# Attention probabilities of the later half blocks: 32x32 block turns on VectorE and a way through DRAM in place of TensorE transposes

## The chip, the cores and the metric

The kernel runs on one core of a Trainium2 chip. The metric is the device time of one execution in microseconds (us); the kernel before takes 675.06 us, the median of three runs (675.04 to 675.08).

## The reference

Four batches of 8 heads, 768 positions and 64 dimensions go through an attention with a window of 16 on either side and 24 block summaries. The result, 3072 tokens of 512, goes through a two-layer network of 512 to 2048 to 512 with a rational function between the layers.

```python
k_sum = k.reshape(B, H, nb, block, D).max(axis=3)          # block = 32, nb = 24
v_sum = v.reshape(B, H, nb, block, D).mean(axis=3)
scores_l = where(|i - j| < 16, scale * q @ k.T, -1e9)
scores_s = scale * einsum('bhsd,bhnd->bhsn', q, k_sum) + log(block)
a = softmax(concatenate([scores_l, scores_s], axis=-1))    # +1e-9 below
x = (a @ concatenate([v, v_sum], axis=2)), heads side by side: [3072, 512]
h = x @ w_in
P = a[0] + a[1]*h + a[2]*h**2 + a[3]*h**3
Q = 1 + |b[0]|*|h| + |b[1]|*h**2
out = (P / (Q + 1e-6)) @ w_out
```

## The kernel before

**Attention.** The 3072 queries are cut into 48 half blocks of 64 (`HQ`). A half block sees `NK` = 120 keys: 96 of its window and 24 summaries. Its scores for all 8 heads stand in one PSUM tile `sc` of 128 rows (2 heads x 64 queries) and 4 x 120 columns (4 head pairs). `scores` (line 195) is a generator in five pieces: TensorE (PE) computes `sc`; VectorE (DVE) adds the mask, scales and takes the smallest value, into `ss` in SBUF; ScalarE (ACT) takes the exponential and the sum `sm`; DVE inverts `sm`; GpSimd (POOL) multiplies `ss` by it. For the product with the values the probabilities must stand with the keys on the partitions: `turned` (line 241) does this with four PE transposes into the PSUM tile `pt`, one per head pair, and `copied` (line 279) has ACT copy `pt` into `pts`. `both_values` (line 284) then multiplies two half blocks by their values `vw` into one tile `av` of PSUM and copies that into the tokens `x`.

**Network.** The tokens go in 6 groups of 512 and each group through 16 steps of 128 hidden columns, 96 steps in all. A step is 12 matmuls for the first layer (`moe1`, tile `h`) and 12 for the second (`moe2`, four tiles `po`), which runs three steps behind (`LAG`). Each layer is three products of parts in high and low precision. Between them `gelu` evaluates the rational function: ACT squares and scales, DVE runs six operations of 128x512 on `tq`, `tu` and `gh`, ACT runs a logarithm and an exponential, and POOL makes `gl`. The PSUM banks of `h` are two, and `av` takes its turn among them; `sc` and `pt` have two of their own, `po` has four.

**Where the two meet.** Half blocks 0 to 15 are done early. The 32 later ones are taken in pairs: the two of a pair are scored at step 14 + 4k (k from 0 to 15) and multiplied by their values four steps later, so one pair falls to every four steps. From step 14 on (`NSTRICT`) a scheduler orders each engine's instructions at build time, with a raised priority for scores, loads and values. The transposes of a pair are put between the second layer's matmuls of the two steps after next: `turned_copied` (line 472) is handed to `moe2` (line 403), which puts one transpose ahead of every three matmuls, the first half block's in step 14 + 4k + 2, the second's one step on. `Kept` (line 75) passes every operation on, so all of them carry its line, 85, and are told apart by their tiles. All loads and stores of this phase are issued by SyncE (SP) in one queue: the next pair's `qw` and `kw` (`att_load`, line 185), its `vw` (`load_v`, line 230), summaries, and the output.

Of the kernel before, what the change touches and what calls it, by code (L numbers as in the profile page):

```python
# [22 lines left out]
P = 128  # L23
# [7 lines left out]
NK = NKW + NB  # L31
NKC = NK // NB
GT = 512
NG = NT // GT
# [16 lines left out]
EARLY_HALF = (0, 1, 3, 4, 6, 7, 9, 10)  # L51
NSTRICT = NFC - 2
STEP = "h3 k0 h0 l0 a0 g1 h1 w2 h1 g1 h3 h0 g0 q0 w2 u g0 q0 w3 g1 h0 w2 w3 P2 v h2"
NHALF = NT // HQ
# [3 lines left out]
def tile_kernel(ctx, tc, qw_in, kraw, kwin, vpad, vred, wio, a, b, cmask, cident, cavg, out):  # L58
# [136 lines left out]
    def scores(jj, early=False):  # L195
# [15 lines left out]
        pool, tag = (gp, "gl") if early and jj % 2 else (pp, "p")  # L211
        ss = pool.tile([P, NPAIR, NK], F32, tag=tag, name=f"ss{jj}")
        sm = sp.tile([P, 2, NPAIR], F32, tag="sm", name=f"sm{jj}")
        for pr in range(NPAIR):
            dve.tensor_tensor_reduce(
                out=ss[:, pr, :], in0=sc[:, pr * NK:(pr + 1) * NK], in1=mt, op0=ALU.add, op1=ALU.min,
                scale=-SCALE, scalar=3.0e38, accum_out=sm[:, 0, pr:pr + 1])
        yield
        for pr in range(NPAIR):
            act.activation(ss[:, pr, :], ss[:, pr, :], AF.Exp, scale=-1.0,  # L220
                           bias=sm[:, 0, pr:pr + 1], accum_out=sm[:, 1, pr:pr + 1])
        act.activation(sm[:, 1, :], sm[:, 1, :], AF.Copy, bias=1e-9)
        yield
        dve.reciprocal(sm[:, 1, :], sm[:, 1, :])
        yield
        for pr in range(NPAIR):
            gps.tensor_scalar(ss[:, pr, :], ss[:, pr, :], sm[:, 1, pr:pr + 1], 1.0, op0=ALU.mult, op1=ALU.mult)
        att[jj] = ss
# [49 lines left out]

    def copied(jj):
        pt = att[jj]  # L280
        att[jj] = pp.tile([NK, NPAIR, P], F32, tag="p", name=f"pts{jj}")
        act.copy(att[jj], pt[:NK, :].rearrange("k (r q) -> k r q", r=NPAIR))

    def both_values(j0):
# [5 lines left out]
        for k in range(2):  # L290
            pts = att.pop(j0 + k)
            for pr in range(NPAIR):
                for e in range(2):
                    pe.matmul(
                        av[e * D:(e + 1) * D, pr, k, :],
                        vw[k][:, (2 * pr + e) * D:(2 * pr + e + 1) * D],
                        pts[:, pr, e * HQ:(e + 1) * HQ], start=True, stop=True)
        act.copy(x32[g][:, :, hh * HQ:(hh + 2) * HQ], av.rearrange("p r k q -> p r (k q)"))
# [104 lines left out]
    def moe2(fc, po, gh, gl, between):  # L403
        wt = weights(fc)
        for t in range(TPG):
            with tc.high_priority(offset=40):
                next(between, None)
            ts_ = slice(t * P, (t + 1) * P)
# [13 lines left out]
    def second_layer(step, queue, po, pt):  # L422
# [7 lines left out]
        return po  # L430

    vnext = tc.dram_tile([NB, DM], F32, name="vnext")
    vres = vw + [mp.tile([NK, DM], F32, tag=t, name=f"vr{i}") for i, t in enumerate(("ta", "tq", "ta", "tq"))]
# [29 lines left out]
    def lead(chain, all_of=False):  # L463
        for _ in chain or ():
            if not all_of:
                return

    def finish_half(jj, early, copy=None):
        lead(turned(jj, early), True)
        return values(jj, early, copy)  # L470

    def turned_copied(jj):
        yield from turned(jj)
        copied(jj)

# [47 lines left out]
    for step in range(NG * NFC + LAG):  # L523
# [54 lines left out]
        with tc.high_priority(offset=40):  # L578
            if step - 4 >= NFC - 2 and halves.get(step - 4):
                both_values(halves[step - 4][0])  # L580
            for jj in halves.get(step, ()):
                key_blocks(jj)
                lead(scores(jj), True)
            for jj in halves.get(step, ()):
                load_v(jj)
                if jj + 2 < NHALF:
                    att_load(jj + 2)
        pt = (z for k in range(2) for jj in halves.get(step - 2 - k, ())[k:k + 1] if jj >= 2 * HPG for z in turned_copied(jj))
        po = second_layer(step, queue, po, pt)
        with tc.high_priority(offset=40):  # L590
            lead(pt, True)
        for f, *args in reduces.get(step, []) + loads.get(step, []):
# [57 lines left out]
```

## Time and profile before

| | before |
|---|---|
| median of 3 runs | 675.06 us |
| the profiled execution's own time | 674.83 us |
| its span, first to last instruction | 673.0 us |
| TensorE clock granted, mean | 0.986 |
| TensorE (PE) busy | 655.2 us, 97% |
| VectorE (DVE) busy | 574.9 us, 85% |
| ScalarE (ACT) busy | 473.7 us, 70% |
| GpSimd (POOL) busy | 263.6 us, 39% |
| DMA | 60.75 MB, mean 90 GB/s |

Busy time is the time in which an engine had an instruction in work. The profiled execution is one run; what lies between its span and its time, 1.8 us, is outside the first and the last instruction.

### The profile page before, as it was taken

How to read it: one execution, taken by the hardware profiler on the slowest of the kernel's cores; microseconds unless marked ns; L12 is line 12 of the kernel's file. 1: busy time of each engine (PE TensorE's matmuls, PEld its weight loads, DVE VectorE, ACT ScalarE, POOL GpSimd, SP SyncE). 2: the span in 40 equal slices, each digit the busy share in tenths (PEclk: the TensorE clock that was granted, in tenths of full speed). 3: DMA queues.
4: the chain of work that ended last, by engine and by line, in shares of the span. 5: the costliest groups of instructions: out<-in, count | busy, mean ns of one | idle time of the engine just before them, and what ended most of it. 6: DMA issues, size and time to landing. Idle time of an engine off the chain costs nothing.

```text
span 673.0 us, 11873 instructions
## 1 busy us (share of the span) xinstructions
PE 655.2 (97%) x4196; PEld 522.7 (78%) x4196; DVE 574.9 (85%) x1116; ACT 473.7 (70%) x1068; POOL 263.6 (39%) x318
## 2 busy tenths in 40 slices
PE   8897989998999999999999999999999999999997
PEld 5675767776878888888888888888788788888886
DVE  4579999998899989977889988878987778988885
ACT  3869879877867668766667677567686576675563
POOL 1736566835334145244244234333442342222221
PEclk9988989999999999999999999999999999999999
DMA  9997644311224302212114222012031000010001
GB/s 322 331 299 243 221 157 146 140 49 62 94 79 118 127 23 70 67 60 64 56 33 132 87 87 69 21 44 63 0 127 64 0 25 1 1 63 1 0 1 63
DMA packets 29671, 60.75 MB, mean 90 GB/s; under 512 B 3636, under 2 KB 15284, under 8 KB 27692
## 3 DMA queue, kind: packets, MB, share of 16 engines
q1 hardware_dynamic: 28908, 59.54, 27.1%
q8 instruction: 33, 0.54, 0.3%
q10 hardware_dynamic: 576, 0.25, 0.2%
q14 instruction: 26, 0.21, 0.1%
q0 software_dynamic: 128, 0.20, 0.1%
HBM read 53.44 MB, written 6.34 MB: 89 GB/s over the span
## 4 chain that ended last, share of the span: by engine, by line
PE 82%; DVE 8%; DMA 3%; ACT 3%; issue 2%; POOL 1%; SPq 0%; DVEq 0%; ACTq 0%
PE po L85 36%; PE h L85 34%; PE sc L85 6%; PE av L85 3%; PE pt L85 3%; DVE tu L85 2%; DMA wr<-in_wio_dram 2%; DVE tq L85 2%; DMA kres<-in_kraw_dram 1%; DVE wr L85 1%; DVE gh L85 1%; PE vf L85 1%; ACT ta L85 1%; ACT ss L85 1%; DVE w L85 1%
## 5 line engine op out<-in xcount | busy, mean ns | idle before, releaser
L85 POOL TENSOR_TENSOR gl<-tu,ta 128x512 fp32r<-128x512 f32 x96 | 128.3, 1337 | 289.9 <-DVE tu L85 159.9
L85 POOL TENSOR_SCALAR ss<-ss,sm 128x120 f32<-128x120 f32 x192 | 107.1, 579 | 101.5 <-DVE sm L85 101.3
L85 DVE SCALAR_TENSOR_TENSOR tq<-tq,cs,ta 128x512 f32<-128x512 f32 x96 | 106.3, 1107 | 38.9 <-ACT ta L85 38.3
L85 ACT ACTIVATE tq<-h 128x512 f32<-128x512 f32 x96 | 57.2, 596 | 107.1 <-PE h L85 104.3
L85 PE MATMUL po<-wearly,gh 128*128 128x512 f32 x384 | 130.2, 421 | 0.0
L85 PE MATMUL po<-w,gh 128*128 128x512 f32 x384 | 126.7, 411 | 0.0
L85 ACT ACTIVATE ta<-tq,cs 128x512 f32<-128x512 f32 x96 | 69.7, 726 | 50.0 <-DVE tq L85 49.5
L85 PE MATMUL h<-xh,wearly 128*128 128x512 f32 x384 | 96.8, 393 | 1.7 <-DVE tu L85 1.1
L85 PE MATMUL h<-xh,w 128*128 128x512 f32 x384 | 95.1, 390 | 0.0
L85 DVE SCALAR_TENSOR_TENSOR gh<-tu,cs,ta 128x512 fp32r<-128x512 f32 x96 | 77.5, 807 | 18.5 <-ACT ta L85 9.9
L85 PEld LDWEIGHTS h<-xh,wearly 128*128 128x128 f32 x384 | 71.7, 188 | 19.9 <-DVE tu L85 1.6
L85 PEld LDWEIGHTS h<-xh,w 128*128 128x128 f32 x384 | 72.1, 188 | 15.5
L85 ACT ACTIVATE ss<-ss,sm 128x120 f32<-128x120 f32 x192 | 73.3, 386 | 10.8 <-DVE sm L85 10.0
L85 PEld LDWEIGHTS po<-wearly,gh 128*128 128x128 f32 x384 | 66.4, 193 | 17.7 <-issue 2.6
L85 PEld LDWEIGHTS po<-w,gh 128*128 128x128 f32 x384 | 65.9, 189 | 16.9 <-issue 1.3
L85 PE MATMUL po<-w,gl 128*128 128x512 f32 x192 | 75.4, 392 | 1.0 <-POOL gl L85 1.0
L85 PE MATMUL po<-wearly,gl 128*128 128x512 f32 x192 | 76.2, 397 | 0.0
L85 ACT ACTIVATE tu<-h,cs 128x512 f32<-128x512 f32 x96 | 74.9, 781 | 0.0
L85 DVE SCALAR_TENSOR_TENSOR tu<-tu,cs,tq 128x512 f32<-128x512 f32 x96 | 72.0, 750 | 2.7
L85 DVE SCALAR_TENSOR_TENSOR tu<-tu,cs,h 128x512 f32<-128x512 f32 x96 | 71.4, 744 | 2.2
L85 DVE SCALAR_TENSOR_TENSOR tq<-tq,gh 128x512 f32<-128x512 f32 x96 | 66.6, 694 | 3.2
L85 ACT ACTIVATE ta<-h,cs 128x512 f32<-128x512 f32 x96 | 65.5, 682 | 4.2 <-POOL gl L85 4.2
(68 smaller groups left out, 972.1 us busy)
## 6 DMA issues: line engine op xcount, KB each, us to landing
wr<-in_wio_dram SPq DMA_DIRECT2D x15, 1024.0 KB, 6.9
vw<-in_vpad_dram SPq DMA_DIRECT2D x42, 192.0 KB, 2.8
kw<-in_kwin_dram SPq DMA_DIRECT2D x40, 192.0 KB, 3.3
out_dram<-o SPq DMA_DIRECT2D x24, 256.0 KB, 2.1
qw<-in_qw_dram SPq DMA_DIRECT2D x40, 128.0 KB, 3.2
kr<-in_kraw_dram SPq DMA_DIRECT2D x12, 384.0 KB, 3.0
vr<-in_vred_dram SPq DMA_DIRECT2D x8, 384.0 KB, 3.4
vf<-in_vpad_dram SPq DMA_DIRECT2D x2, 1024.0 KB, 12.2
```

The lines of the kernel that those rows point to most:

```text
L85: out = getattr(self.engine, name)(*args, **kw)
```

## The change

For the 32 later half blocks `ss` is widened to 128 columns, of which POOL clears the last eight. The two score chains of a pair run piece by piece side by side, where before one followed the other. One step after the scores (`CROSS`) `crossed` has DVE turn `ss` in blocks of 32x32 into `tb`: within each block queries and keys change places, and the blocks stay where they are. To bring the blocks to their rows, `tb` is written to DRAM (`cross`, 256 KB, one of four places in turn) and read back in four pieces, one for each 32 keys (the last 24), each with 64 KB or less in runs of 512 B, into `pts`, which has two buffers of its own. Writes and reads are issued by SP. The matmuls of `both_values` read `pts` as two runs of 32 columns. The PE transposes and ACT copies of these half blocks are gone; the early half blocks keep theirs.

```diff
--- before.py
+++ after.py
@@ -30,6 +30,8 @@
 NKW = HQ + 2 * WIN
 NK = NKW + NB
 NKC = NK // NB
+SQ = 32
+NKB = -(-NK // SQ)
 GT = 512
 NG = NT // GT
 HPG = GT // HQ
@@ -50,6 +52,7 @@
 NSTG = 8
 EARLY_HALF = (0, 1, 3, 4, 6, 7, 9, 10)
 NSTRICT = NFC - 2
+CROSS = 1
 STEP = "h3 k0 h0 l0 a0 g1 h1 w2 h1 g1 h3 h0 g0 q0 w2 u g0 q0 w3 g1 h0 w2 w3 P2 v h2"
 NHALF = NT // HQ
 
@@ -209,22 +212,24 @@
                     pe.matmul(sc[rows, pr * NK + lo:pr * NK + hi], qt[rows, pr, :], k[rows], start=True, stop=True)
         yield
         pool, tag = (gp, "gl") if early and jj % 2 else (pp, "p")
-        ss = pool.tile([P, NPAIR, NK], F32, tag=tag, name=f"ss{jj}")
+        ss = pool.tile([P, NPAIR, P], F32, tag=tag, name=f"ss{jj}")[:, :, 0:NK if jj < 2 * HPG else P]
         sm = sp.tile([P, 2, NPAIR], F32, tag="sm", name=f"sm{jj}")
         for pr in range(NPAIR):
             dve.tensor_tensor_reduce(
-                out=ss[:, pr, :], in0=sc[:, pr * NK:(pr + 1) * NK], in1=mt, op0=ALU.add, op1=ALU.min,
+                out=ss[:, pr, 0:NK], in0=sc[:, pr * NK:(pr + 1) * NK], in1=mt, op0=ALU.add, op1=ALU.min,
                 scale=-SCALE, scalar=3.0e38, accum_out=sm[:, 0, pr:pr + 1])
         yield
         for pr in range(NPAIR):
-            act.activation(ss[:, pr, :], ss[:, pr, :], AF.Exp, scale=-1.0,
+            act.activation(ss[:, pr, 0:NK], ss[:, pr, 0:NK], AF.Exp, scale=-1.0,
                            bias=sm[:, 0, pr:pr + 1], accum_out=sm[:, 1, pr:pr + 1])
         act.activation(sm[:, 1, :], sm[:, 1, :], AF.Copy, bias=1e-9)
         yield
         dve.reciprocal(sm[:, 1, :], sm[:, 1, :])
         yield
+        if jj >= 2 * HPG:
+            gps.memset(ss[:, :, NK:], 0.0)
         for pr in range(NPAIR):
-            gps.tensor_scalar(ss[:, pr, :], ss[:, pr, :], sm[:, 1, pr:pr + 1], 1.0, op0=ALU.mult, op1=ALU.mult)
+            gps.tensor_scalar(ss[:, pr, 0:NK], ss[:, pr, 0:NK], sm[:, 1, pr:pr + 1], 1.0, op0=ALU.mult, op1=ALU.mult)
         att[jj] = ss
 
     def load_v(jj):
@@ -276,10 +281,18 @@
             yield
             dve.tensor_tensor(xl[:, :, cols], av, xh[:, :, cols], op=ALU.subtract)
 
-    def copied(jj):
-        pt = att[jj]
-        att[jj] = pp.tile([NK, NPAIR, P], F32, tag="p", name=f"pts{jj}")
-        act.copy(att[jj], pt[:NK, :].rearrange("k (r q) -> k r q", r=NPAIR))
+    def crossed(jj):
+
+        ss = att[jj]
+        tu = pp.tile([P, NKB, NPAIR, SQ], F32, tag="p", name=f"tb{jj}")
+        dve.transpose(out=tu.rearrange("p n r q -> p r n q"), in_=ss.rearrange("p r (n q) -> p r n q", q=SQ))
+        nc.sync.dma_start(out=cross[jj % 4], in_=tu)
+        att[jj] = pp.tile([NK, P // SQ, NPAIR, SQ], F32, tag="pts", name=f"pts{jj}", bufs=2)
+        for n in range(NKB):
+            k = min(SQ, NK - n * SQ)
+            nc.sync.dma_start(
+                out=att[jj][n * SQ:n * SQ + k],
+                in_=cross[jj % 4][:, n].rearrange("(b a) r q -> a b r q", a=SQ)[0:k])
 
     def both_values(j0):
 
@@ -292,9 +305,9 @@
             for pr in range(NPAIR):
                 for e in range(2):
                     pe.matmul(
-                        av[e * D:(e + 1) * D, pr, k, :],
+                        av[e * D:(e + 1) * D, pr, k, :].rearrange("d (b q) -> d b q", q=SQ),
                         vw[k][:, (2 * pr + e) * D:(2 * pr + e + 1) * D],
-                        pts[:, pr, e * HQ:(e + 1) * HQ], start=True, stop=True)
+                        pts[:, 2 * e:2 * e + 2, pr, :], start=True, stop=True)
         act.copy(x32[g][:, :, hh * HQ:(hh + 2) * HQ], av.rearrange("p r k q -> p r (k q)"))
 
     def split(g):
@@ -404,7 +417,7 @@
         wt = weights(fc)
         for t in range(TPG):
             with tc.high_priority(offset=40):
-                next(between, None)
+                lead(between)
             ts_ = slice(t * P, (t + 1) * P)
             for i, (l, r) in enumerate(((gh, 0), (gh, 1), (gl, 0))):
                 pe.matmul(po[t], l[:, ts_], wt[:, r, 1, :], start=(fc == 0 and i == 0),
@@ -429,6 +442,7 @@
                 finish(g, po)
         return po
 
+    cross = [tc.dram_tile([P, NKB, NPAIR, SQ], F32, name=f"cross{i}") for i in range(4)]
     vnext = tc.dram_tile([NB, DM], F32, name="vnext")
     vres = vw + [mp.tile([NK, DM], F32, tag=t, name=f"vr{i}") for i, t in enumerate(("ta", "tq", "ta", "tq"))]
     vlast = stage.tile([NK, 2, DM], F32, tag="st", name="vlast")
@@ -468,10 +482,6 @@
     def finish_half(jj, early, copy=None):
         lead(turned(jj, early), True)
         return values(jj, early, copy)
-
-    def turned_copied(jj):
-        yield from turned(jj)
-        copied(jj)
 
     def whole(jj):
         yield from scores(jj)
@@ -580,15 +590,18 @@
                 both_values(halves[step - 4][0])
             for jj in halves.get(step, ()):
                 key_blocks(jj)
-                lead(scores(jj), True)
+            chain = [scores(jj) for jj in halves.get(step, ())]
+            for _ in range(5):
+                for c in chain:
+                    lead(c)
+            for jj in halves.get(step - CROSS, ()):
+                if jj >= 2 * HPG:
+                    crossed(jj)
             for jj in halves.get(step, ()):
                 load_v(jj)
                 if jj + 2 < NHALF:
                     att_load(jj + 2)
-        pt = (z for k in range(2) for jj in halves.get(step - 2 - k, ())[k:k + 1] if jj >= 2 * HPG for z in turned_copied(jj))
-        po = second_layer(step, queue, po, pt)
-        with tc.high_priority(offset=40):
-            lead(pt, True)
+        po = second_layer(step, queue, po, None)
         for f, *args in reduces.get(step, []) + loads.get(step, []):
             f(*args)
```

In the following pieces a name ends in a running number; `ss_3320` and `ss_3345` before are `ss_3357` and `ss_3363` in the changed kernel.

On PE, in step 8 of the third group, which is two steps after a pair's scores, this stands before:

```order
L85 MATMUL h_8_3421<-xh_2882,w_1106 128x512 x8
L85 MATMUL h_8_3421<-xl_2883,w_1106 128x512 x4
L85 MATMUL pt_3451<-ident,ss_3320 120x128
L85 MATMUL po_0_3149<-wearly,gh_5_3227 128x512 x2
L85 MATMUL po_0_3149<-wearly,gl_5_3228 128x512
L85 MATMUL pt_3451<-ident,ss_3320 120x128
L85 MATMUL po_1_3150<-wearly,gh_5_3227 128x512 x2
L85 MATMUL po_1_3150<-wearly,gl_5_3228 128x512
```

and this in the changed kernel:

```order
L88 MATMUL h_8_3467<-xh_2920,w_1110 128x512 x8
L88 MATMUL h_8_3467<-xl_2921,w_1110 128x512 x4
L88 MATMUL po_0_3191<-wearly,gh_5_3262 128x512 x2
L88 MATMUL po_0_3191<-wearly,gl_5_3263 128x512
L88 MATMUL po_1_3192<-wearly,gh_5_3262 128x512 x2
L88 MATMUL po_1_3192<-wearly,gl_5_3263 128x512
```

Four such transposes to a half block are gone, 128 in all; nothing else on PE has moved.

On DVE, from the end of step 6 of the same group (`sm` is the two halves' sum, `gh`, `tq` and `tu` with their step's number are the rational function), before:

```order
L85 SCALAR_TENSOR_TENSOR gh_6_3276<-tu_6_3280,cs,ta_6_3278 128x512
L85 SCALAR_TENSOR_TENSOR tq_6_3279<-tq_6_3279,gh_6_3276 128x512
L85 RECIPROCAL sm_3321<-sm_3321 128x4
L85 RECIPROCAL sm_3346<-sm_3346 128x4
L85 SCALAR_TENSOR_TENSOR tu_6_3280<-tu_6_3280,cs,tq_6_3279 128x512
L85 SCALAR_TENSOR_TENSOR tq_7_3395<-tq_7_3395,cs,ta_7_3394 128x512
L85 TENSOR_TENSOR tu_7_3396<-tu_7_3396,h_7_3379 128x512
L85 SCALAR_TENSOR_TENSOR tu_7_3396<-tu_7_3396,cs,h_7_3379 128x512
L85 SCALAR_TENSOR_TENSOR gh_7_3392<-tu_7_3396,cs,ta_7_3394 128x512
```

and now:

```order
L88 SCALAR_TENSOR_TENSOR gh_6_3304<-tu_6_3308,cs,ta_6_3306 128x512
L88 SCALAR_TENSOR_TENSOR tq_6_3307<-tq_6_3307,gh_6_3304 128x512
L88 RECIPROCAL sm_3358<-sm_3358 128x4
L88 RECIPROCAL sm_3364<-sm_3364 128x4
L88 SCALAR_TENSOR_TENSOR tu_6_3308<-tu_6_3308,cs,tq_6_3307 128x512
L88 STREAM_TRANSPOSE tb_3439<-ss_3357 128x4x4x32
L88 SCALAR_TENSOR_TENSOR tq_7_3425<-tq_7_3425,cs,ta_7_3424 128x512
L88 STREAM_TRANSPOSE tb_3447<-ss_3363 128x4x4x32
L88 TENSOR_TENSOR tu_7_3426<-tu_7_3426,h_7_3409 128x512
L88 SCALAR_TENSOR_TENSOR tu_7_3426<-tu_7_3426,cs,h_7_3409 128x512
L88 SCALAR_TENSOR_TENSOR gh_7_3422<-tu_7_3426,cs,ta_7_3424 128x512
```

Two transposes have come in, one on either side of the first operation of step 7, and ahead of the two products `tu` with `h`; the multiplication of `ss` by POOL comes before each.

On SP, from the loads of the next pair's queries and keys, before:

```order
L187 DMA qw_98<-in_qw_dram 128x256
L188 DMA kw_96<-in_kwin_dram 128x384
L187 DMA qw_99<-in_qw_dram 128x256
L188 DMA kw_97<-in_kwin_dram 128x384
L233 DMA vw_100<-in_vpad_dram 96x512
L233 DMA vw_101<-in_vpad_dram 96x512
```

and now:

```order
L190 DMA qw_98<-in_qw_dram 128x256
L191 DMA kw_96<-in_kwin_dram 128x384
L190 DMA qw_99<-in_qw_dram 128x256
L191 DMA kw_97<-in_kwin_dram 128x384
L289 DMA cross_109<-tb_3439 128x512
L289 DMA cross_110<-tb_3447 128x512
L293 DMA pts_3442<-cross_109 32x4x128 x3
L293 DMA pts_3442<-cross_109 24x4x128
L293 DMA pts_3450<-cross_110 32x4x128 x3
L293 DMA pts_3450<-cross_110 24x4x128
L238 DMA vw_100<-in_vpad_dram 96x512
L238 DMA vw_101<-in_vpad_dram 96x512
```

Two writes and eight reads stand between those loads and the loads of the values; the writes wait for DVE, and the first read of each tile for its write's landing.

## Rows read from the trace of the kernel before

**Rows 1.** Part 1 of the page: busy us (share of the span) xinstructions of each engine

```profile
PE 655.2 (97%) x4196; PEld 522.7 (78%) x4196; DVE 574.9 (85%) x1116; ACT 473.7 (70%) x1068; POOL 263.6 (39%) x318
```

**Rows 2.** Chain that ended last, one period: start us, us, what

```profile
201.00 1.08 PE av L85 x32
202.09 1.79 PE sc L85 x32
203.87 2.95 PE po L85 x12
206.82 2.72 PE h L85 x12
209.54 2.72 PE po L85 x12
...
214.99 0.11 PE pt L85
215.10 0.70 PE po L85 x3
```

**Rows 3.** Busy time by stretch of one period: each engine's us, then clock and DMA

```profile
149.08:175.04 25.96, 23.84 (x106) 18.06 (x106) 23.27 (x51) 19.49 (x45) 10.96 (x13) 1.00 0.18 56
...
201.00:226.96 25.96, 25.96 (x171) 21.07 (x172) 24.78 (x47) 17.62 (x41) 8.73 (x12) 1.00 0.34 103
226.96:252.92 25.96, 25.96 (x171) 21.08 (x172) 23.21 (x49) 17.29 (x41) 8.74 (x12) 1.00 0.23 71
252.92:278.88 25.96, 25.96 (x171) 21.07 (x172) 24.07 (x47) 19.49 (x45) 12.72 (x14) 1.00 0.15 46
...
356.76:382.72 25.96, 25.96 (x171) 21.08 (x172) 24.94 (x49) 19.37 (x45) 10.63 (x12) 1.00 0.35 100
...
460.60:486.56 25.96, 25.96 (x171) 21.08 (x172) 23.28 (x46) 19.59 (x45) 11.14 (x12) 1.00 0.14 41
...
sum 389.40, PE 389.40 PEld 316.18 DVE 332.73 ACT 273.56 POOL 141.87; mean PE 25.96 PEld 21.08 DVE 22.18 ACT 18.24 POOL 9.46
```

**Rows 4.** All instructions of tile pt: ns min/median/max, first and last start us

```profile
L85 PE MATMUL pt<-ident,ss x192: 270/271/469, 17.9 to 560.8; 128*120 128x128 f32 x192
```

**Rows 5.** DVE groups by form, 201 to 564 us: busy, mean ns | idle before

```profile
L85 DVE SCALAR_TENSOR_TENSOR tq<-tq,cs,ta 128x512 f32<-128x512 f32 x56 | 61.1, 1091 | 29.9 <-ACT ta L85 29.7
...
L85 DVE TENSOR_TENSOR tu<-tu,h 128x512 f32<-128x512 f32 x56 | 37.9, 677 | 0.0
```

**Rows 6.** The same view over the whole run

```profile
L85 DVE MEMSET zero<- 128x512 f32 x1 | 0.5, 485 | 0.9 <-PEq L639 0.9
```

**Rows 7.** DVE in order of time: start us, us, instruction [idle before <-releaser]

```profile
280.13 1.39 DVE L85 SCALAR_TENSOR_TENSOR tq<-tq,cs,ta 128x512 f32<-128x512 f32 x1 [0.60 <-ACT ta L85]
...
289.22 0.75 DVE L85 SCALAR_TENSOR_TENSOR tq<-tq,cs,ta 128x512 f32<-128x512 f32 x1 [0.88 <-ACT ta L85]
289.95 0.69 DVE L85 TENSOR_TENSOR tu<-tu,h 128x512 f32<-128x512 f32 x1
```

**Rows 8.** POOL in order of time, the same stretch

```profile
279.70 1.27 POOL L85 TENSOR_TENSOR gl<-tu,ta 128x512 fp32r<-128x512 f32 x1 [3.07 <-DVE tu L85]
...
288.27 3.30 POOL L85 TENSOR_SCALAR ss<-ss,sm 128x120 f32<-128x120 f32 x8
```

**Rows 9.** DVE in order of time, a period with a value reduction

```profile
224.54 0.75 DVE L85 SCALAR_TENSOR_TENSOR tu<-tu,cs,h 128x512 f32<-128x512 f32 x1
```

**Rows 10.** DMA issues: x issues, KB each, median us from issue to landing

```profile
out_dram<-o SPq DMA_DIRECT2D x24, 256.0 KB, 2.1
qw<-in_qw_dram SPq DMA_DIRECT2D x40, 128.0 KB, 3.2
...
vr<-in_vpad_dram SPq DMA_DIRECT2D x4, 192.0 KB, 12.5
```

**Rows 11.** SP in order of time: start us, us, issue

```profile
279.54 0.80 SPq L233 DMA_DIRECT2D vw<-in_vpad_dram  x2
...
281.37 0.42 SPq L188 DMA_DIRECT2D kw<-in_kwin_dram  x1
```

## The prediction

> **What bounds the kernel now.** I read the shares of the engines first, then the chain of waits over one period, then the busy time period by period, and last the order in time around the places that change. TensorE is busy for 97% of the span and VectorE for 85% [rows 1], so a saving on the one is a load on the other, and where each stands matters. From the second pair of half blocks on the work repeats every four steps, in 25.96 us. The chain of such a period is all PE: the values of one pair, 1.08 us; the scores of another, 1.79; a second layer of 2.95; first and second layers of 2.72 each; and, in two of the second layers, four transposes that hold the chain for 0.11 us each and stretch the three matmuls behind them to 0.70 [rows 2], where three matmuls of an undisturbed layer take 2.72 / 4 = 0.68. The stretches say the same: in each of the 15 periods from 175.04 to 564.44 us PE is busy for all of 25.96 us, 389.40 in sum, at the full granted clock, and VectorE for 22.18 in the mean [rows 3]. So in these 389 us nothing but PE counts, and VectorE has 3.8 us to spare per period in the mean, but far less in some: 24.78, 23.21 and 24.07 in three that follow one another, 24.94 and 23.28 in two more [rows 3]. These hold reductions of keys and values and the splits of a new group. The period before, in which the first pair's transposes stand, has PE busy for 23.84 of 25.96 us [rows 3]: there others are waited for.
>
> **What PE gains.** A transpose takes some 271 ns by itself [rows 4], but most of that lies beside other matmuls; what counts is the chain. Without transposes a period is 1.08 + 1.79 + 2.95 + 7 x 2.72 = 24.86 us, which is 1.10 less than 25.96. For 15 pairs that is 16.5 us. The first pair's gain lies between nothing (PE waits there anyway) and 1.1; I take half, 0.5. Together 17.0, and 674.83 - 17.0 = 657.8 us for the profiled execution, whose time stands 0.23 below the median of the runs; I forecast against it and leave that difference to the range.
>
> **What VectorE pays.** Each half block brings one turn of 128x512. The trace has no such instruction. Nearest is an operation of one output of that size, `tu` times `h`, at 677 ns; a clearing of the same size, which reads nothing, took 485 ns, the lower end [rows 5, 6]. I know nothing that makes a turn dearer than twice a product, 1.35 us, and take that as the upper end, the product as the value: in, out and elements are as many. To the work comes a wait. Replay the period from 278.88: POOL begins the eight multiplications at 288.27 and ends them at 291.57, 0.41 each, so the first half block's four end at 289.92 [rows 8]. The first turn stands ahead of step 7's `tq`, which began at 289.22, and the second behind it, ahead of `tu` times `h` at 289.95 [rows 7]. Now: first turn 289.92 to 290.59, `tq` to 291.34, second turn from 291.57, when POOL is done, to 292.24, and only then `tu` times `h`. That is 2.3 us later: 1.34 of work and 1.0 of waiting for POOL. Behind it stand the rest of that step's function and the next one's.
>
> Whether PE feels it: it needs the two products with `h` to free a bank of `h`, and `gh` and `gl` three steps later. The three steps cover several microseconds; the bank covers less. In the period to 226.96 the last product ended at 225.29, 1.67 ahead of the values that take its bank [rows 9]; with the 0.54 us that four transposes less bring PE forward, 1.1 is left. Charge every period 2.3: the mean becomes 24.5 of 24.86, which fits, so in a light period the delay is made up before the next pair. The heavy ones exceed 24.86 by 2.22, 0.65 and 1.51 (in a row), 2.38, and 0.72. Take from each run of heavy periods the 1.1 that the bank covers: 3.3 + 1.3 + 0 = 4.6 us lost, if nothing is given back. Something will be: `tq` takes 1.39 us where it runs beside POOL's `gl` and 0.75 where it does not [rows 7, 8], 1.09 in the mean [rows 5]; four of them in a period hold 1.4 us that a later, back-to-back VectorE need not lose, enough for all of the excess. I take the middle, 2.5 us lost, with 0 and 4.6 as ends at this price of a turn.
>
> The Trainium skill speaks against this change: "VectorE: DVE Perf Modes", section "The three transpose paths", gives TensorE 390 ns for 128x128 in bf16 and VectorE 311, the latter in separate blocks of 32x32 only, and its "Rules for kernel authors" leave 128x128 turns to TensorE where PSUM will do as the target. Four such squares would be 1.24 us a half block by that figure (an estimate; the data here are fp32), and the sum some 665 us. In the trace here a transpose on TensorE costs its chain 0.14 us, 1.10 / 8, less than half of the page's figure.
>
> **The transfers.** They lie beside everything, if they land in time. For the same period: second turn done at 292.24, its write issued in some 0.4 us [rows 11] and landed 2.1 later, as the output's stores of the same 256 KB do [rows 10], at 294.7; the first tile's write and reads are through by then or queued ahead on SP; the second tile's four reads are issued one after another at 0.42 us, to 296.5, and land 3.3 us later, a little over the 3.2 of `qw` [rows 10]: 299.8. The values of this pair start on PE at 278.88 + 24.86 = 303.74. That leaves 3.9 us. What is queued on SP behind the writes and reads is the loads of `vw`, which cannot start before the preceding values anyway, next `qw` and `kw`, and stores of the output, whose buffers are needed 16 steps later: no cost. The upper end for a landing is the slowest small load of the trace, 12.5 us [rows 10], at the busy start.
>
> **What I cost at nothing.** ACT loses 32 copies and is busy 18.24 of 25.96 us [rows 3]: off the path on either side of the change. POOL gains 32 clearings of 128x4x8, at 9.46 of 25.96 us busy [rows 3]; they wait only for a buffer and lie in POOL's idle time; if they did not, each would push the turns by less than a multiplication's 0.41. The interleaved score chains bring the first half block's probabilities no later than POOL's order above has them. The values' matmuls read two runs of 32 columns instead of one of 64; the scores already read keys in runs of 24 and run 32 matmuls in 1.79 us [rows 2], so I give it nothing.
>
> Sum: 674.83 - 17.0 + 2.5 = **660.3 us**.
>
> **The rivals.**
> *VectorE becomes the bound.* If a turn costs 1.35 us, a period's charge is 2.3 + 2 x 0.67 = 3.65, the mean 25.8 against 24.86. VectorE then sets the pace in all but the lightest periods. Over the 15 stretches the excess comes to about 16 us after the banks' 1.1 per run of periods; with nothing given back that is 657.8 + 16 = 674, with 1.4 per heavy period given back 661 to 662; I take 668. For it: VectorE's 85%, its FIFO order, and that the turn writes in an order of its own, 32 by 32. Against: rows of 0.68 to 0.75 for every plain operation of that size.
> *Transfers land late, and the kernel gets slower.* The reads come in pieces of 512 B. If they land not 3.3 but over 8.3 us after issue, the 3.9 us of slack and the 1.1 of gain are gone, and each period is longer than before. PE would wait at `av`, and as the next pair's scores stand behind `av`, the delay would come back in each period. At 12.5 us, `av` starts 5.3 late: 15 x 5.3 = 80, and 657.8 + 80 = 738 us. For it: the one row at 12.5. Against: 2.1 to 3.2 us for loads and stores of this phase [rows 10], and DMA engines busy for 0.14 to 0.35 of the stretches shown [rows 3].
> *No effect.* The saved time reappears as waiting of PE on `gl` or `h`, whatever the turn's price, since VectorE's chain after the scores is longer by 2.3 us in every period and no light one makes it up: about 675. Against: PE waits for nothing in 389 us, so VectorE keeps a reserve throughout.
>
> **How the numbers follow.** Forecast 0.60; VectorE as the bound 0.27; late transfers 0.08; no effect 0.05. A measurement of this kernel can tell a change of 0.2%, 1.35 us, so faster means under 673.7 and slower over 676.4. The forecast and nearly all of the second rival are faster: 0.86. Same takes most of no effect and a little of the second: 0.05; slower the rest: 0.09. The range goes from 656.0 (a turn at 485 ns, nothing lost, the first pair's whole 1.1 gained, and the period before it a little shorter) to 671.0, which takes in the middle and the upper part of the second rival and leaves out late transfers, no effect and the tail of VectorE, some 0.17.
>
> **What would show it.** Right: no `pt` after the first sixteen half blocks; a period of 24.9 us in the light stretches, with PE busy throughout; a turn's row near 0.68 us; idle time of VectorE of about 1 us per period ended by POOL's `ss`; waits of PE for VectorE's `tu` or POOL's `gl` of some 2.5 us in sum, near the stretches that are now at 201 to 279 and 357 to 383 us; reads landed 3 us or more ahead of `av`. Wrong: a turn of over 1 us and VectorE busy for over 97% of each period; waits of PE at `av` that a transfer of `pts` ends; or waits for `h` in the light periods too.

## The result and the profile after

The changed kernel takes 665.8 us (median of 4 runs, 665.17 to 666.42), beside 675.05 for the kernel before in the same series (674.99 to 675.08): a ratio of 0.9863, 95% interval 0.9846 to 0.988. That is 9.3 us faster where 14.5 were forecast. The profiled execution took 665.17 us with a span of 663.4.

What follows speaks of periods: the time from the first values matmul of one pair of later half blocks to that of the next. Period 1 begins with the values of the first such pair, at 174.25 us in the changed kernel, and holds the scores and the turns of the second; period 15 ends with the values of the sixteenth, at 554.78. The splits of a new group (`xh` and `xl`) stand in periods 4, 8 and 12. The busy time of each engine by period, for the kernel after (columns as in [rows 3]):

```profile
174.25:200.00 25.75, 25.36 (x161) 20.43 (x161) 21.90 (x46) 18.30 (x43) 9.96 (x14) 1.00 0.42 137
200.00:226.39 26.39, 24.94 (x161) 20.59 (x161) 26.00 (x51) 17.62 (x41) 10.30 (x16) 1.00 0.45 139
226.39:251.25 24.86, 24.86 (x161) 20.59 (x161) 23.59 (x51) 15.96 (x38) 10.12 (x13) 1.00 0.44 132
251.25:277.41 26.16, 25.29 (x161) 20.44 (x161) 23.29 (x46) 19.00 (x44) 11.85 (x16) 1.00 0.28 84
...
351.98:380.69 28.71, 25.23 (x161) 20.52 (x161) 27.63 (x52) 18.56 (x44) 10.69 (x15) 1.00 0.41 126
...
sum 380.53, PE 374.33 PEld 308.50 DVE 340.08 ACT 260.58 POOL 150.59; mean PE 24.96 PEld 20.57 DVE 22.67 ACT 17.37 POOL 10.04
```

Ten of the 15 periods last 24.85 or 24.86 us: the forecast length, to the hundredth. The other five, periods 1, 2, 4, 8 and 12, last 25.75, 26.39, 26.16, 28.71 and 24.95. Against 15 x 24.86 = 372.9 the sum of 380.53 has lost 7.6 us, and half of that in period 8. I call this difference **the loss**; it is the measure for the experiments, since the time at which period 1 begins differs by up to 5 us between profiles (172.66 to 177.23). What makes the difference ahead of it was not looked into.

PE's waits for VectorE in the whole run, changed kernel (what waited, for what: us in total, times, longest):

```profile
PE av L88 <- DVE tu L88: 4.4, 5, 1.7
...
PE h L88 <- DVE tu L88: 3.1, 3, 1.7
```

`tu` is the product with `h`, whose end frees the bank that `av` or the next but one `h` takes. Between 174 and 555 us these waits are 4.4 and 1.9 us, so they are most of the loss. No wait for a transfer of a later `pts` is among PE's waits, and none in these periods for `gl`. Where the longest of them arise is seen on VectorE in period 8:

```profile
362.32 3.00 DVE L88 TENSOR_TENSOR xl<-x,xh 128x512 fp32r<-128x512 f32 x4
365.24 0.77 DVE L88 SCALAR_TENSOR_TENSOR tq<-tq,cs,ta 128x512 f32<-128x512 f32 x1
366.62 0.71 DVE L88 STREAM_TRANSPOSE tb<-ss 128x512 f32<-128x512 f32 x1 [0.61 <-POOL ss L88]
367.25 0.65 DVE L88 TENSOR_TENSOR tu<-tu,h 128x512 f32<-128x512 f32 x1
367.98 0.71 DVE L88 STREAM_TRANSPOSE tb<-ss 128x512 f32<-128x512 f32 x1
368.61 1.17 DVE L88 TENSOR_REDUCE vs<-vr 96x32 f32<-96x1024 f32 x1
369.71 0.73 DVE L88 SCALAR_TENSOR_TENSOR tu<-tu,cs,h 128x512 f32<-128x512 f32 x1
```

Between the first operation of step 47, `tq`, and the second product with `h`, which frees the bank, stand both turns, a wait for POOL and a reduction of values. From the start of `tq` to the end of that product it is 5.2 us, 365.24 to 370.44; the three operations by themselves are 0.75, 0.69 and 0.75 in [rows 7, 9], 2.2. The 3.0 us more are the two turns, 0.63 each from start to start, the wait, 0.6, and the reduction, 1.1. PE waited until 370.49 for this bank, 1.74 us, and ten microseconds later 1.74 once more:

```profile
370.49 2.11 PE L88 MATMUL h<-xh,wearly 128*128 128x512 f32 x8 [1.74 <-DVE tu L88]
...
380.69 1.15 PE L88 MATMUL av<-pts,vw 120*64 120x64 f32 x32 [1.74 <-DVE tu L88]
```

What the first of these turns waited for, on POOL:

```profile
362.85 5.09 POOL L88 TENSOR_SCALAR ss<-ss,sm 128x120 f32<-128x120 f32 x8
```

The eight multiplications took 5.09 us here, beside VectorE's four `xl`, where the light period of [rows 8] had 3.30. The turns themselves, over the whole run (ns: min/median/max), and VectorE's idle time before them (us, times):

```profile
L88 DVE STREAM_TRANSPOSE tb<-ss x32: 696/711/715, 158.8 to 541.5; 128x512 f32<-128x512 f32 x32
...
  POOL ss L88: 13.8, 22
```

### The profile page after: what moved, and what is told of

It reads as the page before. It is cut to its first block, busy times and chain, and to the rows that moved or that the text cites. A ratio compares the mean times of both kernels' runs of the same rounds, so it can differ in the third digit from the quotient of the medians.

```text
span 663.4 us, 11846 instructions
## 1 busy us (share of the span) xinstructions
PE 637.9 (96%) x4068; PEld 513.1 (77%) x4068; DVE 582.9 (88%) x1148; ACT 459.9 (69%) x1036; POOL 272.3 (41%) x350
## 4 chain that ended last, share of the span: by engine, by line
PE 63%; DVE 19%; ACT 6%; POOL 5%; issue 4%; DMA 2%; SPq 0%; DVEq 0%; POOLq 0%; ACTq 0%
PE po L88 29%; PE h L88 27%; DVE tu L88 6%; DVE tq L88 5%; PE sc L88 4%; POOL ss L88 3%; DVE gh L88 3%; PE av L88 3%; ACT ss L88 2%; ACT ta L88 2%; DMA kres<-in_kraw_dram 1%; DVE ks L88 1%; DVE ss L88 1%; PE pt L88 1%; DVE wr L88 1%
## 5 line engine op out<-in xcount | busy, mean ns | idle before, releaser
L88 POOL TENSOR_TENSOR gl<-tu,ta 128x512 fp32r<-128x512 f32 x96 | 133.8, 1393 | 283.1 <-DVE tu L88 184.0
L88 PE MATMUL po<-wearly,gh 128*128 128x512 f32 x384 | 124.7, 407 | 0.0
L88 PE MATMUL po<-w,gh 128*128 128x512 f32 x384 | 120.4, 395 | 0.0
L88 DVE SCALAR_TENSOR_TENSOR tq<-tq,cs,ta 128x512 f32<-128x512 f32 x96 | 98.1, 1022 | 15.2 <-ACT ta L88 14.8
L88 DVE SCALAR_TENSOR_TENSOR gh<-tu,cs,ta 128x512 fp32r<-128x512 f32 x96 | 74.1, 772 | 12.0 <-ACT ss L88 3.0
L88 PEld LDWEIGHTS po<-wearly,gh 128*128 128x128 f32 x384 | 71.4, 193 | 16.6 <-issue 2.8
L88 PEld LDWEIGHTS po<-w,gh 128*128 128x128 f32 x384 | 70.8, 188 | 15.7 <-issue 1.3
L88 DVE SCALAR_TENSOR_TENSOR tq<-tq,gh 128x512 f32<-128x512 f32 x96 | 69.1, 719 | 2.7
```

The lines of the kernel that those rows point to most:

```text
L88: out = getattr(self.engine, name)(*args, **kw)
```

## The experiments

The expectations name these theories. **A**: the loss comes from the turns in VectorE's queue, where VectorE is heavily loaded. It splits into **A1**, that VectorE's amount of work per period decides, **A2**, that the place decides, turns with their wait for POOL ahead of the product that frees a bank, and **A3**, that this wait alone does. **B**: the loss comes from the transfers. **C**: it comes from the interleaved score chains.

### Without the turns

```diff
-        tu = pp.tile([P, NKB, NPAIR, SQ], F32, tag="p", name=f"tb{jj}")
-        dve.transpose(out=tu.rearrange(...), in_=ss.rearrange(...))
-        nc.sync.dma_start(out=cross[jj % 4], in_=tu)
+        nc.sync.dma_start(out=cross[jj % 4].rearrange("p n r q -> p (n r q)"), in_=ss.rearrange("p r k -> p (r k)"))
```

> VectorE's turns of the later half blocks are left out: the probabilities are written to DRAM as they are, so what comes back is not turned. Score chains, writes, reads and everything else stay. Theory A (the 7.7 us that the periods lose beyond 24.86 us come from the turns in VectorE's queue, by their work and their wait for POOL, in the periods that are heavy for VectorE): all 15 periods near 24.86, about 658 us (657 to 659.5). Theory B (they come from the transfers, by a wait or by contention): still 664 to 667. Theory C (they come from the interleaved score chains and the new order of VectorE): 663 to 667.

Measured: 659.7 us (658.62 to 660.2). The loss is 1.4 us: 374.26 for the 15 periods, from 175.48 to 549.74. Fourteen of them stand at 24.85 to 24.88; what is left is in period 8:

```profile
349.50:375.71 26.21, 24.93 (x162) 20.59 (x161) 25.41 (x49) 19.66 (x46) 10.78 (x15) 1.00 0.45 128
```

So the turns, with their wait for POOL, account for 6.3 of the 7.6 us. The other 1.4 stand in a period in which VectorE is busy for 25.41 us, more than 24.86, with no turn in it; its four `xl` take 976 ns each there, 722 before. The transfers were all there.

### The score chains one after the other

```diff
-            chain = [scores(jj) for jj in halves.get(step, ())]
-            for _ in range(5):
-                for c in chain:
-                    lead(c)
+            for jj in halves.get(step, ()):
+                lead(scores(jj), True)
```

> Only the interleaving of the two score chains is undone: one half block's chain is written out in full and then the other's; turns and transfers stay. Theory A: within 1.5 us of the changed kernel's 665.8. Theory B: the same. Theory C: 658 to 662.

Measured: 665.75 us (665.24 to 665.96), the loss 7.7, period 8 again 28.71 us. C falls.

### Without the transfers

```diff
-        nc.sync.dma_start(out=cross[jj % 4], in_=tu)
-        att[jj] = pp.tile([NK, P // SQ, NPAIR, SQ], F32, tag="pts", name=f"pts{jj}", bufs=2)
-        for n in range(NKB):
...
+        att[jj] = tu[0:NK]
```

> The turns stay, the writes to DRAM and the reads back are left out: the values' matmuls read the turned tile as it lies, 120 rows of it, so its blocks are in the wrong rows. Theory A: within 1.5 us of 665.8, since the transfers land ahead of their use. Theory B: 657 to 660. Theory C: within 1.5 us of 665.8.

Measured: 665.61 us (664.45 to 667.46), the loss 7.7: 380.58 for the periods, against 380.53. B falls. In the changed kernel's light period the issues on SP (start us, us) stand here:

```profile
290.14 1.58 SPq L289 DMA_DIRECT2D cross<-tb  x2
292.19 3.53 SPq L293 DMA_DIRECT2D pts<-cross  x8
```

The last read is issued at 295.72 and the values begin at 302.26, 6.5 us later. The landing has no row in this trace. In the run with the turns behind the product (below) the reads of `pts` have one, 1.8 to 3.7 us after issue, with a median of 2.0.

### The turns twice

```diff
+        dve.transpose(out=tu.rearrange("p n r q -> p r n q"), in_=ss.rearrange("p r (n q) -> p r n q", q=SQ))
         nc.sync.dma_start(out=cross[jj % 4], in_=tu)
```

> Each turn is done twice, into the same tile. That is 0.63 to 0.71 us more per half block, 1.3 to 1.4 per pair. Theory A: the light periods have over 2.9 us of VectorE free and stay at 24.86; the heavy ones (four to six) pay most of 1.4 each: 6 to 9 us more, 671 to 675. Theory B: under 1.5 us more than 665.8, as the transfers start only 0.7 us later. Theory C: under 1.5 us more. If VectorE were the bound everywhere: 16 x 1.4 = 22 us more, 688.

Measured: 680.84 us (678.42 to 681.83), slower than the kernel before (ratio 1.008, 1.0049 to 1.0111). The loss is 21.0 us: 13.4 more for 15 x 1.3 to 1.4 us of added work, two thirds of it, and more than A had said. The surprise is a light period: the seventh takes 26.65 us though VectorE is free for 2.25 of them:

```profile
337.97:364.62 26.65, 24.92 (x160) 20.59 (x161) 24.40 (x48) 16.56 (x40) 8.98 (x15) 1.00 0.36 108
```

On VectorE, in that period:

```profile
349.18 1.75 DVE L88 SCALAR_TENSOR_TENSOR tq<-tq,cs,ta 128x512 f32<-128x512 f32 x1
...
352.06 0.69 DVE L88 STREAM_TRANSPOSE tb<-ss 128x512 f32<-128x512 f32 x1
352.68 0.90 DVE L88 TENSOR_REDUCE ks<-kr 128x24 f32<-128x768 f32 x1
353.51 0.73 DVE L88 SCALAR_TENSOR_TENSOR tu<-tu,cs,h 128x512 f32<-128x512 f32 x1
```

Again turns and a reduction stand ahead of the product that frees the bank. PE waits 1.73 us, ten microseconds later, for the bank of the next values: the delay was not made up by then. An amount of work below the period's 24.86 us was not enough here; hence A1 against A2. VectorE's waits are no part of that amount, and before the first of these turns it waited 1.29 us for POOL.

### The turns behind the product

`released` keeps the name of each step's second product with `h`; the dependence sets an order and adds no wait, since both are on VectorE.

```diff
+    def behind(out, step):
+        tc.add_manual_dep(out.ins, released[step], ORDERED, reason="behind the bank")
...
+        turn = dve.transpose(...)
+        behind(turn, start_of(jj) + CROSS)
...
+            ins = dve.scalar_tensor_tensor(out=tu, in0=tu, scalar=cs[:, 1:2], in1=h, ...)
+            released[g * NFC + fc] = ins.ins.name
```

> Both turns of a pair are ordered behind the second product of tu with h of their step, the one that frees the bank of h, by a dependence that only orders. Nothing is added or removed. Theory A1 (what counts is VectorE's work in the heavy periods: they hold more than 24.86 us of it, wherever the turns stand): within 1.5 us of 665.8, the loss over the 15 periods still 6 us or more. Theory A2 (what counts is the place: turns, and their wait for POOL, stand ahead of the product that frees the bank, while gh and gl behind it have 5 us and more to spare): the loss falls from 7.7 to 2 to 3 us, 660 to 661.5. If the turns come too late for the transfers, PE waits for pts in every period and the time rises.

Measured: 665.41 us, the loss 7.1. The four runs took 663.8, 664.15, 666.67 and 666.82; the profiled one, to which the loss belongs, is the longest. By the median A1 is right; by the periods each is right in part. Periods 1 and 4, which had lost 0.9 and 1.3, are at 24.86, and period 2 is down from 1.5 to 1.0. Period 8 is not helped, 28.51 us, and now its waiting is one piece of 3.58 us. Behind that piece a new loss of 2.5 us appears: period 9 takes 27.37 us with PE busy throughout. PE in order of time there:

```profile
379.90 1.98 PE L88 MATMUL av<-pts,vw 120*64 120x64 f32 x32 [3.58 <-DVE tu L88]
381.81 3.47 PE L88 MATMUL sc<-kw,qw 64*64 64x120 f32 x32
```

[Rows 2] have 1.08 and 1.79 for these. The granted clock (the number before the last two) of the stretch before the wait, of the wait and of what follows:

```profile
351.39:376.00 24.61, 24.61 (x161) 20.58 (x160) 24.23 (x48) 16.93 (x41) 9.42 (x13) 1.00 0.44 133
376.00:379.90 3.90, 0.32 (x3) 0.00 (x1) 3.86 (x6) 2.72 (x5) 1.69 (x2) 0.83 0.34 101
379.90:383.00 3.10, 3.10 (x44) 2.98 (x46) 3.03 (x5) 2.54 (x5) 0.00 (x0) 0.50 0.25 68
383.00:386.00 3.00, 3.00 (x27) 2.61 (x24) 2.96 (x12) 0.58 (x3) 1.27 (x1) 0.60 0.61 175
386.00:390.00 4.00, 4.00 (x19) 3.26 (x19) 1.96 (x13) 4.00 (x19) 1.03 (x4) 1.00 0.30 88
```

After the wait the clock was at its lower level, 1.2 GHz, and came back to 2.4 in the stretch from 383 to 386. Without these 2.5 us the loss is 4.6, which is above the 2 to 3 of A2. The move also took the turns' wait for POOL away: it is 0.3 us in the whole run, once, against 13.8 in 22 times. So as a whole this run does not tell the place from that wait.

### The reductions moved

```diff
-        s = max(start_of(bi * NJ) - SOFF, 0)
+        s = max(start_of(bi * NJ) - (0, 12, 9, 16)[bi], 0)
```

> The key and value reductions of the third batch are begun three steps later, those of the fourth four steps earlier, so that fewer of them stand in the periods in which a group is split; the turns stand as the scheduler puts them. Theory A1: period 8 (now 28.71 us) loses 1 to 1.5 instead of 3.85, period 2 under 1 instead of 1.53, the lighter neighbours stay within 0.3 of 24.86: 661.5 to 663.5. Theory A2: less than that, 663.5 to 666, since the turns still stand ahead of the product.

Measured: 667.63 us (665.91 to 669.42), the loss 9.7. Both theories missed. Period 8 comes down to 27.91 us, by less than A1 had said, and periods 2, 3, 7 and 12 go up to 26.99, 26.88, 26.07 and 25.61. The moved reductions push up their neighbours, the third period among them, which had 1.3 us of VectorE free. Of that period's loss 1.7 us lie in PE being busy for 26.57 us: it begins after a wait of 2.07, with a granted clock of 0.71 and 0.74 in its first six microseconds. Without these 1.7 the loss would be 8.0, still not below the changed kernel's.

### Both edits

> The edits of the two preceding runs together: turns behind the product, reductions moved. Theory A1: as the moved reductions alone, 661.5 to 663.5. Theory A2: 658.5 to 660.5, the best of all, near the 657.8 that PE alone would give.

Measured: 664.2 us (661.86 to 665.87), the loss 5.0: above what either theory had said. Periods 2 and 12 are back at 24.86; periods 3, 4, 7 and 8 take 25.91, 25.44, 25.56 and 27.48. The reductions still stood eight in a row, one per step; the runs from the spread reductions on change that.

### ACT multiplies

```diff
-            gps.tensor_scalar(ss[:, pr, 0:NK], ss[:, pr, 0:NK], sm[:, 1, pr:pr + 1], 1.0, op0=ALU.mult, op1=ALU.mult)
+            act.activation(ss[:, pr, 0:NK], ss[:, pr, 0:NK], AF.Copy, scale=sm[:, 1, pr:pr + 1])
```

(for the later half blocks only)

> The eight multiplications of a pair's probabilities by the inverted sums are done by ACT instead of POOL; the turns stay where the scheduler puts them. That takes away the turns' wait for POOL (13.8 us of VectorE's idle time in all) and POOL's work beside VectorE, and gives ACT some 3 us more per pair, of the 7 it has free. If the wait for POOL is what the turns cost (theory A3): the 15 periods lose 2 us or less, 659 to 661. If it is the turns' work and place (A1, A2): 663 to 666. If ACT's added work delays the function's chain: over 667.

Measured: 664.71 us (662.81 to 665.01), the loss 5.9. That is in the 663 to 666 of A1 and A2 and not in the 659 to 661 of A3. Period 8 is down to 27.01 us, but the twelfth is up from 24.95 to 26.03. The turns still waited, only for ACT, as VectorE's idle time before them shows:

```profile
  ACT ss L88: 10.4, 18
```

Against the 13.8 us for POOL that is little less, so over the whole run the price of the wait is not told from that of the place. In period 8 the turns waited for nothing, and it still lost 2.15 us: there A3 is not the whole cause.

### The reductions spread

The third batch's eight reductions go to steps 18, 20, 21, 23, 24, 26, 27 and 29, the fourth's to 34, 36, 37, 39, 40, 42, 43 and 45, their loads one step ahead.

```diff
-            reduces.setdefault(s + k + 1, []).append((key_sum, bi, k))
+            reduces.setdefault(when[k], []).append((key_sum, bi, k))
...
-            reduces.setdefault(s + NPAIR + k + 1, []).append((value_sum, bi, k))
+            reduces.setdefault(when[NPAIR + k], []).append((value_sum, bi, k))
```

> The eight reductions of keys and values of the third and the fourth batch are spread over 12 steps each instead of eight in a row (steps 18 to 29 and 34 to 45), so that none stands beside the split of a group; the turns stand where the scheduler puts them. The sum over the 15 periods is what is compared: the changed kernel loses 7.7 us there against 15 x 24.86. Theory A1 (VectorE's work per period decides): period 8 loses 0 to 1 us instead of 3.85, no period over 1, a sum of 2 to 3.5: 660.5 to 662.5 in the median. Theory A2 (only the place of the turns counts): a sum of 5.5 or more: 663.5 to 666.

Measured: 663.43 us (661.66 to 664.23), the loss 5.1: between the two bands. Period 2 loses 1.5, and period 8 still 1.8 with only 23.77 us of VectorE in it:

```profile
351.94:378.59 26.65, 25.57 (x162) 20.43 (x161) 23.77 (x50) 18.54 (x44) 11.48 (x14) 1.00 0.25 79
```

What its loss comes from stands on VectorE:

```profile
363.47 0.71 DVE L88 STREAM_TRANSPOSE tb<-ss 128x512 f32<-128x512 f32 x1 [0.86 <-POOL ss L88]
364.10 1.74 DVE L88 TENSOR_TENSOR xl<-x,xh 128x512 fp32r<-128x512 f32 x2
365.77 0.77 DVE L88 SCALAR_TENSOR_TENSOR tq<-tq,cs,ta 128x512 f32<-128x512 f32 x1
367.48 0.71 DVE L88 STREAM_TRANSPOSE tb<-ss 128x512 f32<-128x512 f32 x1 [0.94 <-POOL ss L88]
...
368.80 0.75 DVE L88 SCALAR_TENSOR_TENSOR tu<-tu,cs,h 128x512 f32<-128x512 f32 x1
```

The first turn and its wait stand between the second and the third `xl`, and PE's four matmuls on `xl` take 1.47 us there instead of 1.07. The second stands ahead of the product, which ends 3.8 us after `tq` begins; PE waits 0.45 us for that bank and 0.53 for the next. So here place and wait cost time in a period whose work would fit.

### Spread, and the turns behind the product

> The spread reductions and, besides, both turns ordered behind the product of their step that frees the bank. If place and work each count where the other does not (periods 1 and 4 by place, 8 by work), the sum over the 15 periods is 0 to 1.5 us and the time 658.5 to 661; if one of them alone counts, it equals the spread reductions alone or the moved turns alone (a loss of 4.6 without the slow clock).

Measured: 659.7 us (657.86 to 661.51), a ratio of 0.9748 to the kernel before, 0.9716 to 0.978, which lies clear of the changed kernel's interval: this version beats both. The loss is 0.5 us, all in period 6, as expected if place and work each count:

```profile
299.81:325.15 25.34, 24.93 (x161) 20.59 (x160) 23.35 (x46) 16.58 (x40) 9.32 (x15) 1.00 0.48 129
350.00:374.86 24.86, 24.86 (x161) 20.58 (x160) 24.06 (x50) 18.64 (x43) 10.76 (x14) 1.00 0.27 84
```

In periods 4 and 8 VectorE has 0.8 us free and PE waits for nothing. The place that cost most, now:

```profile
362.25 0.77 DVE L88 SCALAR_TENSOR_TENSOR tq<-tq,cs,ta 128x512 f32<-128x512 f32 x1
362.94 0.68 DVE L88 TENSOR_TENSOR tu<-tu,h 128x512 f32<-128x512 f32 x1
363.65 0.75 DVE L88 SCALAR_TENSOR_TENSOR tu<-tu,cs,h 128x512 f32<-128x512 f32 x1
364.32 1.38 DVE L88 STREAM_TRANSPOSE tb<-ss 128x512 f32<-128x512 f32 x2
```

It is 2.15 us instead of 5.2 from the start of `tq` to the bank, and in the whole run no turn waits for POOL. Neither edit gives this alone (losses of 4.6 without the slow clock, and 5.1): with both, 7.2 of the 7.6 us come back.

### The same, and ACT multiplies

> As the run before, and ACT instead of POOL multiplies a pair's probabilities by the inverted sums. VectorE then no longer runs beside those multiplications and the turns no longer wait for them: a sum over the 15 periods of 0 to 1 us, 658 to 660.5. If ACT's 3 us more per pair delay the function's logarithm and exponential: over 661, with waits of PE for VectorE's tu behind ACT.

Measured: 665.01 us (663.74 to 667.48), the loss 5.6, of which 5.1 in periods 4, 8 and 12, those of the group splits: 26.33, 26.33 and 27.06 us. That is the expectation's second case. VectorE is busy for 23.65 us of the last of them and waits for ACT. Its groups there:

```profile
L88 DVE SCALAR_TENSOR_TENSOR tq<-tq,cs,ta 128x512 f32<-128x512 f32 x4 | 5.0, 1238 | 1.5 <-ACT ta L88 1.5
...
L88 DVE TENSOR_TENSOR xl<-x,xh 128x512 fp32r<-128x512 f32 x4 | 2.5, 690 | 1.3 <-ACT xh L88 1.3
```

The split's copies and the multiplications share ACT's queue with the function's logarithm. The 7 us that ACT had free in a period of the changed kernel did not show whether its queue could take more work in time.

### The kernel before, reductions spread

> The kernel before, with its TensorE transposes, and only the reductions spread. By theory A1 VectorE's heavy periods cost nothing as long as a period is 25.96 us long, so spreading them gains nothing: within 1 us of the kernel before, all 15 periods still 25.96. If the reductions hurt by themselves in the kernel before, it is faster by 1 us or more.

Measured: 675.38 us (672.9 to 680.14), a ratio of 0.9999, 0.9971 to 1.0027; all 15 periods 25.96. What costs time in the changed kernel cost nothing before, as long as PE was full.

## Why the prediction was right, and where it was off

The sign and the range held: 665.8 lies in 656 to 671. The forecast of 660.3 was 4.9 us under the profiled run's 665.17, and one term of the sum accounts for it.

- **PE's gain**: right. Periods of 24.86 us, 1.10 less than before, 16.5 over 15.
- **The first pair**: 0.5 forecast; period 1 begins 0.7 earlier than in the trace before, within what profiles differ there, so this is not decided.
- **The turn's price**: 0.68 forecast, 0.71 measured. The wait for POOL: 1.0 a pair forecast; 13.8 us over 16 pairs measured, 0.9. That the wait came out is in part luck. The replay laid the order of step 7, which belongs to period 6, on the rows of period 5. In period 5 of the changed kernel the turns run behind the first product with `h` and wait for nothing; in period 6 both stand ahead of it, and the first waits for 1.28 us, the second for 0.27:

```profile
311.58 0.71 DVE L88 STREAM_TRANSPOSE tb<-ss 128x512 f32<-128x512 f32 x1 [1.28 <-POOL ss L88]
```

- **The loss**: 2.5 forecast, with 0 and 4.6 as ends; 7.6 measured, outside both. This is the term that was mis-sized, "Whether PE feels it". It took the 2.3 us of delay from a light period and charged the heavy ones only by the sum of their work, less 1.1 for the bank's cover, less what a back-to-back VectorE gives back. Its list of heavy periods also lacks two that its own charge takes above 24.86, periods 1 and 9 (VectorE at 22.89 and 22.83), by 0.33 and 0.27; with them the upper end would be 5.2. The first of them:

```profile
175.04:201.00 25.96, 25.96 (x171) 21.09 (x172) 22.89 (x46) 19.58 (x45) 9.34 (x13) 1.00 0.34 112
```

By periods, 2 to 4 lost 2.8 us, within the 3.3 of the upper end. What went beyond it stands in two others. Period 1 lost 0.9 where nothing was charged. Its turns, here with their neighbours left out, wait for nothing, and with the turns behind the product it is back at 24.86, so this is the place by itself:

```profile
186.16 0.70 DVE L88 STREAM_TRANSPOSE tb<-ss 128x512 f32<-128x512 f32 x1
...
188.02 0.70 DVE L88 STREAM_TRANSPOSE tb<-ss 128x512 f32<-128x512 f32 x1
```

And period 8 lost 3.85 where the upper end has 1.3. Two things were wrong for period 8. The delay is larger there: POOL's multiplications take 5.09 instead of 3.30 us, and with turns, wait and a reduction the bank comes free 5.2 us after `tq` begins instead of 2.2. And nothing is given back there. Over the whole run the relief came: `tq` has a mean of 1022 ns after, against 1107 before, over 96 instructions 8.2 us. But in period 8 `tq` was fast already and grew slower, and another group, `tu` from `tq`, grew more. The period holds four of each in both kernels; before:

```profile
L85 DVE SCALAR_TENSOR_TENSOR tq<-tq,cs,ta 128x512 f32<-128x512 f32 x4 | 3.6, 889 | 0.2 <-ACT ta L85 0.2
...
L85 DVE SCALAR_TENSOR_TENSOR tu<-tu,cs,tq 128x512 f32<-128x512 f32 x4 | 3.0, 757 | 0.0
```

and in the changed kernel:

```profile
L88 DVE SCALAR_TENSOR_TENSOR tu<-tu,cs,tq 128x512 f32<-128x512 f32 x4 | 3.9, 976 | 0.1
L88 DVE SCALAR_TENSOR_TENSOR tq<-tq,cs,ta 128x512 f32<-128x512 f32 x4 | 3.7, 920 | 0.0
```

With the two turns VectorE is busy there for 27.63 us instead of 24.94. The slow multiplications could have been read before, from the same period:

```profile
364.36 5.51 POOL L85 TENSOR_SCALAR ss<-ss,sm 128x120 f32<-128x120 f32 x8 [5.41 <-DVE sm L85]
```

The Trainium skill has a rule for POOL's slow multiplications: by "SBUF — State Buffer", section "Who interferes with whom", a VectorE instruction with two inputs in SBUF, as `xl` has them, contends with a GpSimd instruction that reads SBUF. The trace agrees: the eight multiplications take 5.09 to 5.20 us in the three periods with `xl`, and 3.17 to 4.54 in the other twelve. The turns make 6.3 of the loss, as their omission shows; the rest is period 8, 25.41 us of VectorE without any turn in a period that should last 24.86.
- **The transfers**, the interleaved chains, ACT and POOL's clearings at nothing: right, as far as shown. Taking the transfers out or undoing the chains moves the 15 periods by 0.05 us, and none of PE's waits in them is for ACT or POOL.
- **The rivals**: VectorE as the bound was right in that all of PE's waits in these periods are for VectorE, and wrong in its reason: a turn does not cost 1.35 us, and ten periods lose nothing. Late transfers and no effect did not come. The sum by the price of the Trainium skill ("VectorE: DVE Perf Modes", section "The three transpose paths"), some 665 us, came out near the measured time by luck: a half block's turn takes 0.71 us here, and not the 1.24 estimated from that price.

What stays open: how much of the loss, outside period 1, is the wait for POOL and how much the place, since each run that moved the turns behind the product took that wait away too; and what slows POOL's multiplications to 4.54 us in periods 3 and 9, which hold no `xl`.

## What to carry to other kernels

Work taken off a full engine came back as time here only as far as the next engine's fullest stretch let it: replay the change there and not in a light stretch, with the order that this stretch has and with what runs beside it. Where added work shares a queue with the instruction that frees a scarce buffer, try it behind that instruction; here the scheduler often put it ahead. Place and load had to be mended together: with one of them a loss of 4.6 or 5.1 us stayed, with both 0.5.

## What was not expected of the hardware

A PE wait can cost twice: once as waiting, and again by the clock. After a wait of 3.58 us the granted clock was 0.50 and the next 64 matmuls took 5.3 us instead of 2.9; the period that followed was 2.5 us too long with PE busy throughout. After one of 2.07 us in another run it was 0.71. After one of 2.56 us, in the run with both edits, it stayed at 1.00 and the next period took 24.88 us. So the length of a wait alone does not tell, and what else decides was not tried.
